# Choice's transpose in a PSUM bank of its own, the first tile's x transposed earlier, and scatters at another place in a pair

## The chip, the cores and the metric

The kernel runs on one core of a Trainium2 chip, as one launch. The metric is the time of that launch on the device, in microseconds; the median of several runs is given.

## What is computed

Three layers follow one another. The first is a retention attention over 8 batches, 8 heads, 576 positions and 64 elements a head. Its result, 4608 rows of 512, goes through a mixture of 8 experts, one for each row, and that result through a soft mixture with 32 slots. Cut to what matters:

```python
Dmat = np.where(rel >= 0, gamma[:, None, None] ** rel, 0.0)
attn = ((scale * q @ k.T) * Dmat) @ v                       # 8 x 8 x 576 x 64
x = attn.transpose(0, 2, 1, 3).reshape(4608, 512)
...
logits = x @ w_gate + modality_bias[modality_id]; e_idx = argmax(logits)
gate_w = softmax(logits)[e_idx]
x = gate_w * (relu(x @ w1[e_idx]) @ w2[e_idx])              # 512 -> 1024 -> 512
...
logits = x @ phi                                            # 4608 x 32
slot_input = softmax(logits, over rows).T @ x               # 32 x 512
slot_out = relu(slot_input @ w1[e]) @ w2[e]                 # 4 slots an expert
out = softmax(logits, over slots) @ slot_out
```

## The kernel before

**Attention.** The 4608 rows are 36 tiles of 128, taken in 18 pairs (a, b). In a pair `emit_v` scales the values (POOL, `vh`, L176), `emit_S`, `emit_cross`, `emit_AV`, `emit_state` and `emit_x` make the rows, `emit_tok` (L226, L227) turns the tile of two pairs ago and writes it to `xd` in DRAM, and `emit_gate` (L222, L223) makes the router's logits. Groups of 4 tiles are then routed by chains of small VectorE instructions that `tick` issues a few at a time: argmax, the rank of a row among the rows of its expert (`rank`, matmuls L253 to L255), the place in the sorted table. `scatter(k)` (POOL, L268, an indirect DMA behind a small memset) writes a tile's row numbers to the table `tb`. There are 36 scatters.

**Slots.** The sorted table is then worked through in slots of 128 rows of one expert; 39 slots are in use. `places` loads a piece of `tb`, `gather` (POOL, L315, L316) fetches the rows into one of three tiles `xg`, `emit_xT` (L464, L466) turns them on TensorE and splits them in a hi part (ScalarE) and a lo part (VectorE), in `xl`. `emit_L1` (L475) is the slot's frame: 24 matmuls of 128x512, with the work of the two slots before hung between them at numbered places (`at(n, ...)`). The places that matter are A = 3 and B = 10. For slot i they issue:

- `emit_hT(i-1)` (L484, L485): turns the hidden layer of the slot before; ScalarE copies one half to hT, VectorE the other.
- `emit_l2(i-1)` (L490): the logits of the soft mixture's choice, `wcur` against hT, into columns 256 to 383 of the PSUM tile `ps_m`, which is one bank.
- `emit_sel(i-2)` (L495) and `emit_zT(i-2)` (L505): choice's maximum and the transpose of z, both into `psz(1)`, columns 384 to 511 of the same `ps_m`.
- `emit_z(i-2)`: `p` (VectorE, L508), `cm` (L509, L510), `cx` (ScalarE's exponential, L511), `cy` (POOL, L514), and the scatter of `cy` to `cs` in DRAM (L515).
- `emit_G(i-2)` (L518): `p` against the hidden layer, into the bank `ps_g`, added up in `Gs` by VectorE (L519).

At place B the order is `emit_l2(i-1)` after `emit_z(i-2)`, then `emit_G(i-2)`. From slot 6 on, a branch (`flush`, L544) in which TensorE, ScalarE and VectorE meet stands between zT and z; it does its work only where the expert changes: `Gs` is turned and multiplied by w2, and `W_mm` (L276) and `W_tr` (L279) make the next `wcur` out of `WT`, 2 MB of w2 from DRAM. Loads of the next expert's weights (`raw`, `wt`, `xw`, `w`) are issued on SP's queue around it, and `cast` and `losplit` (L114, L117) split them into `wh` and `wl`.

**Order of the work.** All of it is written by hand: each engine takes its instructions in the order of the code. The tile framework adds the waits between engines, as it finds them from the tiles that instructions share; the rows of the order below show them in brackets.

**Drain.** After the last slot `drain` finishes the two slots in flight and loads what the soft mixture's second part (`layer1`, `layer2`, `emit_y`) needs that no buffer had room for before; the rest of it was loaded in the slots by `piece`.

Of the kernel before, what the change touches and what calls it, by code (L numbers as in the profile page):

```python
# [17 lines left out]
NPF=6  # L18
# [63 lines left out]
def body(nc,tc,I,O):  # L82
# [8 lines left out]
    with ctx, tc.manual_schedule():  # L91
# [11 lines left out]
        xg2=P0.tile([128,DM],F32,name="xg2"); gT=P0.tile([128,256],F32,name="gT"); SI=P0.tile([128,DM],F32,name="SI")  # L103
        wcur,wnext,wt=(P0.tile([128,256],F32,name=x) for x in ("wcur","wnext","wt"))
# [209 lines left out]
        def gather(i,n=NTOK):  # L314
            g=gi.pop(i); u=uis[i%6]; G_.tensor_copy(out=u,in_=g[:,0:1])  # L315
            G_.indirect_dma_start(out=xg[i%3],out_offset=None,in_=xd[0:n],in_offset=bass.IndirectOffsetOnAxis(ap=u,axis=0),bounds_check=n-1,oob_is_err=False)  # L316
            gi[i]=(g,u)
        def early_places():
            for i in range(NE): places(i,rege(i,TC-1))
        def early_gathers():  # L320
            for i in range(NE): gather(i,6*S)
        emit_v(0); emit_S(0); emit_state(0)
        for P_ in range(NT//2-1):
            a,b=2*P_,2*P_+1; ready=rq and rq[0].__name__=="rank"
            loads(a); loads(b)
# [45 lines left out]
        t8=U(E); ic=U(NSLOT); tg=U(NSLOT); b1=U(NSLOT); n36=wt[0:E,0:36]; r4x=wt[0:E,64:64+4*NSLOT]; r4=r4x.rearrange("p (a b) -> p a b",a=4)  # L371
# [59 lines left out]
        PFt=[[RB if (k,h)==(NPF-1,1) else PF.tile([128,2048],F32,name=f"m{k}_{h}") for h in range(2)] for k in range(NPF)]  # L431
# [30 lines left out]
        def emit_xT(i):  # L462
            ps=ring("ps_xT",0,1,[128,4,128],pl=PX)
            for c in range(4): PE.transpose(out=ps[:,c],in_=xg[i%3][:,c*128:c*128+128],identity=ident)  # L464
            hi=ring("xhi",i,2,[128,4,128],F32R); lo=ring("xlo",i,2,[128,4,128],F32R)
            A.copy(out=hi,in_=ps); V.tensor_tensor(out=lo,in0=ps,in1=hi.bitcast(F32),op=ALU.subtract)  # L466
            xT[i]=(hi,lo)
# [115 lines left out]
        def table(at):  # L583
            at(5,lambda: (mm_r4(),go(c_table)))
            at(14,lambda: [places(j,reg(j,0,[ET.SP],TC-1)) for j in range(NE,6)])
            at(15,lambda: (load_raw(NE),next_WT(NE)))
            at(16,lambda: [gather(j) for j in range(NE,6)])
        def busy(n):
            for _ in range(n): PE.matmul(out=ring("ps_L",0,2,[128,512],pl=PX)[:,0:128],lhsT=sel,rhs=ident,start=True,stop=True)  # L589
        emit_xT(0)  # L590
        for i in range(NSURE):
            slot(i)
            x,h=divmod(i-12,2)
            if 0<=x<NPF: piece(x,[h])
            elif 0<=x-NPF<2 or x==NPF+2 and h==0: SP.dma_start(out=mx[x-NPF][:,2048*h:2048*h+2048],in_=half(MX[x-NPF],h))
        n=nc.values_load(tot[0:1,0:1],engines=[ET.PE,ET.Activation,ET.DVE,ET.Pool,ET.SP],min_val=0,max_val=NSLOT,skip_runtime_bounds_check_because="it is a sum of counts")
        siT=P0.tile([128,4,32],F32,name="siT")
        def drain(i):
# [5 lines left out]
            SP.dma_start(out=XW,in_=half(NPF+3,1))  # L604
# [26 lines left out]
        hT2=[PFt[3][0][:,0:1024].rearrange("p (b f) -> p b f",b=8),WT[1][:,0:1024].rearrange("p (b f) -> p b f",b=8)]  # L631
# [76 lines left out]
```

## Time and profile before

| | |
|---|---|
| median of 3 runs | 699.01 us (697.84 to 699.71) |
| profiled run | 696.97 us, of which the span of the core's work is 695.2 us |
| TensorE busy | 589.1 us, 85% of the span |
| VectorE / POOL / ScalarE busy | 320.2 / 247.0 / 192.7 us |
| granted clock of TensorE, mean | 0.95 |
| attention, slots, drain and second part | to about 184 us, 184 to 601 us, 601 us to the end |

Busy shares are means over stages. What a change in one stage is worth is read from the waits of that stage. All times in the rows further down are counted from the start of the span of the profiled run.

### The profile page before, as it was taken

The page shows a single profiled execution, that of the slowest core. Times are in us where ns is not written, and L with a number is a line of the kernel's source. Part 1 is how long each engine was busy: PE and PEld are TensorE (multiplying, and loading weights), DVE is VectorE, ACT ScalarE, POOL GpSimd, SP SyncE. Part 2 cuts the span into 40 slices and gives each one's busy share as a digit, 9 for nine tenths or more (in the row PEclk, how much of TensorE's full clock was granted, in tenths as well). Part 3 has the DMA queues.
Part 4 walks back from the last instruction along what each step waited for, and adds up shares of the span by engine and source line. Part 5 has one row for each costly group of instructions (what it writes and reads, how often), then busy time and mean ns, then how long its engine had stood idle before and what let it go on. Part 6 is the DMA issues. An engine that isn't in the chain of part 4 may idle for free. (4 is left out here: it accounts for less than half of the span.)

```text
span 695.2 us, 17056 instructions
## 1 busy us (share of the span) xinstructions
PE 589.1 (85%) x5913; PEld 446.0 (64%) x5913; DVE 320.2 (46%) x938; ACT 192.7 (28%) x489; POOL 247.0 (36%) x348
## 2 busy tenths in 40 slices
PE   7889899889798898888988889888779988677984
PEld 5678677777566776666766666566656666453454
DVE  2446445555644444454444563344563444332243
ACT  1132122223412222222222442322442322111333
POOL 3532744444743233333333462243462143110000
PEclk8989999999999999999999989999999999979995
DMA  8999968878316110114333389833475300379978
GB/s 307 402 385 394 362 204 289 293 255 305 113 54 258 32 36 20 35 35 156 135 100 141 135 329 356 347 110 134 138 267 209 140 25 5 135 272 342 390 261 283
DMA packets 45518, 142.33 MB, mean 205 GB/s; under 512 B 11972, under 2 KB 23887, under 8 KB 34128
## 3 DMA queue, kind: packets, MB, share of 16 engines
q1 hardware_dynamic: 39632, 130.44, 51.3%
q0 software_dynamic: 5760, 10.33, 4.7%
q8 instruction: 64, 1.05, 0.6%
q14 instruction: 62, 0.51, 0.2%
HBM read 315.99 MB, written 27.71 MB: 494 GB/s over the span
## 5 line engine op out<-in xcount | busy, mean ns | idle before, releaser
L475 PE MATMUL ps_L<-wh,xl 128*128 128x512 f32 x624 | 214.9, 415 | 2.9 <-DVE xl L466 1.8
L475 PEld LDWEIGHTS ps_L<-wh,xl 128*128 128x128 f32 x624 | 117.2, 193 | 43.9 <-issue 16.8
L475 PE MATMUL ps_L<-wl,xl 128*128 128x512 f32 x312 | 126.0, 404 | 0.0
L514 POOL TENSOR_SCALAR cy<-cx,cm 128x32 f32<-128x32 f32 x39 | 14.5, 371 | 176.8 <-DVE cm L513 171.5
L479 DVE TENSOR_SCALAR hh<-ps_L,gi 128x512 f32<-128x512 f32 x39 | 29.3, 750 | 99.4 <-PE ps_L L475 99.3
L490 PE MATMUL ps_m<-xr__79,wcur 128*32 128x128 f32 x624 | 26.1, 287 | 57.2 <-ACT cx L511 56.2
L475 PEld LDWEIGHTS ps_L<-wl,xl 128*128 128x128 f32 x312 | 60.2, 193 | 13.1 <-issue 0.2
L187 DVE TENSOR_TENSOR st_s<-ps_s,cm 128x512 f32<-128x512 f32 x72 | 46.2, 684 | 37.4 <-PE ps_s L184 25.3
L490 PEld LDWEIGHTS ps_m<-xr__79,wcur 128*32 128x32 f32 x624 | 15.1, 111 | 70.8 <-ACT cx L511 69.3
L499 ACT ACTIVATE z<-ps_m,mt 32x128 f32<-32x128 f32 x39 | 13.9, 358 | 140.9 <-DVE mt L498 133.6
L176 POOL TENSOR_TENSOR vh<-kqv,vtab 128x512 f32<-128x512 f32 x28 | 29.0, 1041 | 59.0 <-PE ps_x L213 42.8
L213 PE MATMUL ps_x<-st_s,vh 128*64 128x128 f32 x576 | 44.1, 283 | 6.8 <-issue 6.5
L515 POOL DMA_INDIRECT cs<-cy,ui x39 | 41.7, 1070 | 15.1 <-POOL cy L514 13.2
L478 ACT ACTIVATE hh<-ps_L,gi 128x512 f32<-128x512 f32 x39 | 26.9, 690 | 72.3 <-PE ps_L L475 68.6
L213 PEld LDWEIGHTS ps_x<-st_s,vh 128*64 128x64 f32 x576 | 33.1, 140 | 19.2 <-issue 18.9
L268 POOL DMA_INDIRECT tb<-m x36 | 35.2, 976 | 26.0 <-DVE m L264 12.8
L484 PE MATMUL ps_h<-cs__113,hh 128*128 128x128 f32 x312 | 40.9, 273 | 1.1 <-DVE hh L479 0.8
L218 DVE TENSOR_TENSOR xT<-ps_x,gt 128x512 f32<-128x512 f32 x36 | 23.2, 686 | 38.2 <-PE ps_x L213 38.0
L316 POOL DMA_INDIRECT xr__79<-xd,ui x28 | 31.0, 1107 | 17.1 <-PE ps_L L475 11.0
L227 ACT COPY xr<-ps_t 128x512 f32<-128x512 f32 x36 | 19.9, 588 | 60.3 <-PE ps_t L226 34.7
L484 PEld LDWEIGHTS ps_h<-cs__113,hh 128*128 128x128 f32 x312 | 35.4, 141 | 1.7 <-DVE hh L479 1.1
L184 PE MATMUL ps_s<-kqv 64*128 64x128 f32 x448 | 34.0, 293 | 0.0
(253 smaller groups left out, 963.5 us busy)
## 6 DMA issues: line engine op xcount, KB each, us to landing
raw<-in_w SPq DMA_DIRECT2D x75, 1024.0 KB
w<-in_w SPq DMA_DIRECT2D x36, 2048.0 KB
xw<-in_w2T SPq DMA_DIRECT2D x36, 1024.0 KB
wt<-in_w2T SPq DMA_DIRECT2D x36, 1024.0 KB
kqv<-in_qkv SPq DMA_DIRECT2D x20, 1024.0 KB
m<-in_m SPq DMA_DIRECT2D x19, 1024.0 KB
w<-in_qkv SPq DMA_DIRECT2D x8, 1024.0 KB
xd<-xr SPq DMA_DIRECT2D x32, 256.0 KB
```

The lines of the kernel that those rows point to most:

```text
L176: G_.tensor_tensor(out=t,in0=kqv[g][:,2].rearrange("p (h d) -> p h d",h=H),in1=bc(vtab[:,pos_(g)],[128,H,D],2),op=ALU.mult)
L184: r=slice(64*h,64*h+64); PE.matmul(out=pss[h][:,p],lhsT=pk(g,0)[r,p],rhs=pk(g,1)[r,p],start=True,stop=True)
L187: V.tensor_tensor(out=st,in0=pss[h],in1=bc(masks[g%NCH],[128,NP,128],1),op=ALU.mult)
L213: PE.matmul(out=xo(g,p,h),lhsT=v[:,2*p+h],rhs=sts[g,h][:,p],start=False,stop=p>1,skip_group_check=True)
L268: nodep(G_.indirect_dma_start(out=tb,out_offset=bass.IndirectOffsetOnAxis(ap=idx[:,k:k+1],axis=0),in_=gk[:,k],in_offset=None),"tb")
L316: G_.indirect_dma_start(out=xg[i%3],out_offset=None,in_=xd[0:n],in_offset=bass.IndirectOffsetOnAxis(ap=u,axis=0),bounds_check=n-1,oob_is_e ...
L475: PE.matmul(out=ps,lhsT=a[:,c],rhs=w[h][:,s],start=n==0,stop=n==11); n+=1; m+=1
L478: if h==0: A.activation(out=d,in_=q,func=AF.Relu,scale=g)
L479: else: V.tensor_scalar(out=d,in0=q,scalar1=0.0,scalar2=g,op0=ALU.max,op1=ALU.mult)
L484: for c in range(4): PE.transpose(out=ps[:,c],in_=hh[i%2][:,2*half+c//2,(c%2)*128:(c%2)*128+128],identity=ident)
L490: PE.matmul(out=ps[32*j:32*j+32],lhsT=w[:,hf*128+32*j:hf*128+32*j+32],rhs=t[:,2*j+hf],start=hf==0,stop=hf==1)
L515: nodep(G_.indirect_dma_start(out=cs,out_offset=bass.IndirectOffsetOnAxis(ap=gi[i][1],axis=0),in_=y,in_offset=None,bounds_check=NTOK-1,oob ...
```

## The change

- `psz(1)` is no longer a part of `ps_m`: it is a PSUM tile `ps_z` of its own, in a bank that was free. `emit_sel` and `emit_zT` write there and `emit_z` reads there.
- The kernel no longer sets the size of the scratch for the descriptors of indirect DMAs (8192), but takes the default.
- `scatter`: 3 of a pair (4 once) are issued right behind the pair's two `emit_v`, where 4 stood at the pair's end. The 12 of the last three groups come one after the other: 8 just ahead of the slots, 4 in the first slot, with nothing of POOL's between.
- The first tile's `emit_xT(0)` stands in the last pair, behind `W_mm`; `cast(1)` a pair earlier; `losplit(1)` wholly on POOL, behind the first gathers; the rank of the last group but one behind the gate; `mm_r4` and `c_table` at place 4 of the second slot, not 5.
- Tiles are packed to make room: `xg2`, `gT`, `wcur`, `wnext` and `wt` in one tile (`m6`, seen as `m_81` below), `xr` in a part of `xr_`. The piece `m3_1` (1 MB) has no buffer of its own any more: it takes `WT[1]` and is loaded in the drain, ahead of `XW`, not in the slots.

```diff
-        xg2=P0.tile([128,DM],F32,name="xg2"); gT=P0.tile([128,256],F32,name="gT"); SI=P0.tile([128,DM],F32,name="SI")
-        wcur,wnext,wt=(P0.tile([128,256],F32,name=x) for x in ("wcur","wnext","wt"))
+        M6=P0.tile([128,1536],F32,name="m6"); xg2=M6[:,0:DM]; gT,wcur,wnext,wt=(M6[:,DM+256*j:DM+256*j+256] for j in range(4)); SI=P0.tile([128,DM],F32,name="SI")
...
-            xr=A1.tile([128,DM],F32,name="xr",bufs=2); A.copy(out=xr,in_=xp)
+            xr=XR[:,1024+DM*(g%2):1024+DM*(g%2)+DM]; A.copy(out=xr,in_=xp)
...
             emit_v(b); emit_v(a+2)
+            if a>13:
+                for _ in range(4 if a==30 else 3):
+                    if scat: scatter(scat.pop(0))
...
             tick(14)
-            if a>13:
-                for _ in range(4):
-                    if scat: scatter(scat.pop(0))
...
-                cast(0); losplit(0,[0,1],V); losplit(0,[2,3],G_)
+                cast(0); losplit(0,[0,1],V); losplit(0,[2,3],G_); cast(1)
...
-        emit_v(b); early_gathers(); emit_S(a); emit_cross(a); emit_cross(b)
+        emit_v(b); early_gathers(); losplit(1,range(4),G_); emit_S(a); emit_cross(a); emit_cross(b)
...
-        emit_tok(a-2); emit_tok(b-2); tick(6); emit_S(b); emit_gate(a//2-1); cast(1); losplit(1,[0],V); losplit(1,[1,2,3],G_)
-        emit_AV(a); emit_AV(b); emit_x(a); emit_x(b)
-        tick(20); logit(a-2); logit(b-2); tick(1,False)
-        W_mm(PS1.tile([128,256],F32,name="ps_w",tag="ps_s0")); emit_tok(a); emit_tok(b); emit_gate(a//2,True)
-        W_tr(PS1.tile([128,256],F32,name="ps_wt",tag="ps_s1"),[wcur])
-        tick(20)
-        while scat: scatter(scat.pop(0))
+        emit_tok(a-2); emit_tok(b-2); tick(7); emit_S(b); emit_gate(a//2-1)
+        emit_AV(a); emit_AV(b); emit_x(a); emit_x(b); tick(20)
+        W_mm(PS1.tile([128,256],F32,name="ps_w",tag="ps_s0")); emit_xT(0,PS1.tile([128,4,128],F32,name="ps_xT0",tag="ps_s1"))
+        logit(a-2); logit(b-2); emit_tok(a); emit_tok(b); emit_gate(a//2,True); tick(1,False)
+        W_tr(PS1.tile([128,256],F32,name="ps_wt",tag="ps_s0"),[wcur])
...
-        def psz(j,w=128): return psm[:,256+128*j:256+128*j+w]
+        def psz(j,w=128): return (ring("ps_z",0,1,Z,pl=PX) if j else psm[:,256:384])[:,:w]
...
-            at(5,lambda: (mm_r4(),go(c_table)))
+            at(4,lambda: (mm_r4(),go(c_table)))
...
-        emit_xT(0)
+        tick(20)
+        while scat: scatter(scat.pop(0))
...
-            if 0<=x<NPF: piece(x,[h])
+            if 0<=x<NPF: (x,h)==(3,1) or piece(x,[h])
...
-            SP.dma_start(out=XW,in_=half(NPF+3,1))
+            piece(3,[1]); SP.dma_start(out=XW,in_=half(NPF+3,1))
...
-    nc=bacc.Bacc("TRN2",target_bir_lowering=False,num_devices=1,dynamic_dma_scratch_size=8192)
+    nc=bacc.Bacc("TRN2",target_bir_lowering=False,num_devices=1)
```

In the order of the changed kernel, lines have moved: L505 is L502 there, L490 is L487, L518 is L515, L475 is L472, L464 is L320, L544 is L541, and L253, L276, L279 and L222 are one less. The rows name the line, the matmul's output and inputs, its shape, and in brackets the engines whose semaphores it waits for (Activation is ScalarE, Pool is POOL).

TensorE at place B of an ordinary slot with the branch, before: the last L1 matmul ahead of it, zT, `l2`, `G`, and L1 again.

```order
L475 MATMUL ps_L_2497<-wh_69,xl 128x512
L505 MATMUL ps_m<-cs__113,z_2505 128x128 [waits DVE_49]
L490 MATMUL ps_m<-xr__79,wcur 32x128 [waits Activation_49]
L490 MATMUL ps_m<-xr__79,wcur 32x128 x7
L518 MATMUL ps_g_2508<-hh_2486,p_2493 32x257
L544 UNCONDITIONAL_BRANCH
L518 MATMUL ps_g_2508<-hh_2486,p_2493 32x257 x3
L475 MATMUL ps_L_2497<-wh_69,xl 128x512
```

The same place in the changed kernel (`m_81` is `wcur` in the packed tile).

```order
L472 MATMUL ps_L_2442<-wh_69,xl 128x512
L502 MATMUL ps_z_2447<-cs__109,z_2451 128x128 [waits DVE_49]
L487 MATMUL ps_m<-xr__79,m_81 32x128 [waits Activation_49]
L487 MATMUL ps_m<-xr__79,m_81 32x128
L487 MATMUL ps_m<-xr__79,m_81 32x128 [waits DVE_49]
L487 MATMUL ps_m<-xr__79,m_81 32x128 x5
L515 MATMUL ps_g_2454<-hh_2431,p_2438 32x257 [waits DVE_49]
L541 UNCONDITIONAL_BRANCH
L515 MATMUL ps_g_2454<-hh_2431,p_2438 32x257 x3
L472 MATMUL ps_L_2442<-wh_69,xl 128x512
```

zT now writes `ps_z`, and `l2`'s waits are spread over two of its matmuls. `G` waits for VectorE by itself.

TensorE between attention and slots, before: the last tiles are turned, gated, `W_tr` is made, and the first tile's x is turned and meets L1.

```order
L226 MATMUL ps_t<-cs__113,xT 128x128 x8
L222 MATMUL ps_m<-xT,wg 32x256 x4
L279 MATMUL ps_wt<-cs__113,wt 128x128 [waits Activation_49]
L279 MATMUL ps_wt<-cs__113,wt 128x128
L464 MATMUL ps_xT_2509<-cs__113,xr__79 128x128 [waits DMASW4_49,PE_49]
L464 MATMUL ps_xT_2509<-cs__113,xr__79 128x128 x3
L475 MATMUL ps_L_2497<-wh_69,xl 128x512 [waits Activation_49]
L475 MATMUL ps_L_2497<-wh_69,xl 128x512 [waits DVE_49]
```

In the changed kernel the first tile's x is turned behind `W_mm`.

```order
L275 MATMUL ps_w<-wt_77,phi 32x256 x7
L320 MATMUL ps_xT_2360<-cs__109,xr__79 128x128 [waits DMASW0_49,PE_49]
L320 MATMUL ps_xT_2360<-cs__109,xr__79 128x128 x3
L232 MATMUL ps_m<-cs__109,ls 128x8 [waits Activation_49]
L232 MATMUL ps_m<-cs__109,ls 128x8
L225 MATMUL ps_t<-cs__109,xT 128x128 [waits DVE_49]
L225 MATMUL ps_t<-cs__109,xT 128x128 x3
L225 MATMUL ps_t<-cs__109,xT 128x128 [waits DVE_49]
L225 MATMUL ps_t<-cs__109,xT 128x128 x3
L221 MATMUL ps_m<-xT,wg 32x256 x4
```

The end of the same stretch in the changed kernel, from `W_tr` (its input is `wt` in the packed tile) to the first L1 matmuls.

```order
L278 MATMUL ps_wt<-cs__109,m_81 128x128 [waits PE_49]
L278 MATMUL ps_wt<-cs__109,m_81 128x128
L472 MATMUL ps_L_2442<-wh_69,xl 128x512 [waits PE_49]
L472 MATMUL ps_L_2442<-wh_69,xl 128x512 [waits DVE_49]
L232 MATMUL ps_m<-cs__109,m_81 128x8 [waits DVE_49]
L232 MATMUL ps_m<-cs__109,m_81 128x8
```

Four transposes (L464, now L320) have moved from between `W_tr` and L1 to behind `W_mm`, ahead of the last tiles; the rank's matmuls, which stood ahead of `W_mm`, now stand between the gate (L221) and `W_tr`.

## Rows read from the trace of the kernel before

**Rows 1.** the page's head, and TensorE's busy time (share) and instructions.

```profile
span 695.2 us, 17056 instructions
...
PE 589.1 (85%) x5913; PEld 446.0 (64%) x5913; DVE 320.2 (46%) x938; ACT 192.7 (28%) x489; POOL 247.0 (36%) x348
```

**Rows 2.** waits, 203 to 600 us: engine, line, releaser: us in total, times, longest.

```profile
PE ps_m L490 <- ACT cx L511: 52.1, 37, 3.0
...
DVE p L508 <- PEq L544: 8.2, 25, 0.3
```

**Rows 3.** timeline of TensorE, one slot: start, length (us), [idle before, releaser].

```profile
280.35 0.27 PE L505 MATMUL ps_m<-cs__113,z 128*128 128x128 f32 x1
281.85 0.65 PE L490 MATMUL ps_m<-xr__79,wcur 128*32 128x128 f32 x16 [1.23 <-ACT cx L511]
282.31 0.62 PE L518 MATMUL ps_g<-hh,p 128*32 128x257 f32 x8
```

**Rows 4.** timeline of VectorE, ScalarE and POOL in the same slot.

```profile
279.21 0.69 DVE L485 COPY xr__79<-ps_h 128x512 f32<-128x512 f32 x1
...
280.82 0.19 DVE L508 COPY p<-ps_m 128x32 f32<-128x32 f32 x1 [0.32 <-PEq L544]
...
281.61 0.19 ACT L511 ACTIVATION_READ_ACCUMULATOR cx<-ps_m,cm 128x1 f32 x1
...
282.37 0.37 POOL L514 TENSOR_SCALAR cy<-cx,cm 128x32 f32<-128x32 f32 x1 [4.83 <-DVE cm L513]
```

**Rows 5.** timeline of VectorE and TensorE in the last slot.

```profile
618.86 0.19 DVE L508 COPY p<-ps_m 128x32 f32<-128x32 f32 x1 [0.76 <-PE ps_m L505]
...
619.11 0.64 PE L518 MATMUL ps_g<-hh,p 128*32 128x257 f32 x8 [0.28 <-DVE p L508]
```

**Rows 6.** timeline of TensorE, a slot without the branch.

```profile
221.42 0.64 PE L490 MATMUL ps_m<-xr__79,wcur 128*32 128x128 f32 x16 [1.06 <-ACT cx L511]
```

**Rows 7.** timeline of TensorE, an expert change and the drain.

```profile
413.02 0.64 PE L490 MATMUL ps_m<-xr__79,wcur 128*32 128x128 f32 x16 [3.05 <-ACT cx L511]
...
612.74 1.08 PE L490 MATMUL ps_m<-xr__79,wcur 128*32 128x128 f32 x16 [4.12 <-ACT cx L511]
```

**Rows 8.** timeline of TensorE and VectorE, from attention to the slots.

```profile
179.89 0.18 PE L253 MATMUL ps_m<-m 128*128 128x32 bf16 x1 [0.95 <-DVE m L247]
...
185.46 0.50 PE L475 MATMUL ps_L<-wh,xl 128*128 128x512 f32 x1 [1.04 <-ACT xl L466]
187.79 0.49 PE L475 MATMUL ps_L<-wh,xl 128*128 128x512 f32 x1 [1.83 <-DVE xl L466]
...
187.11 0.63 DVE L466 TENSOR_TENSOR xl<-ps_xT,xl 128x512 fp32r<-128x512 f32 x1
```

**Rows 9.** windows: busy us of each engine, granted clock, DMA share, GB/s.

```profile
400.00:405.00 5.00, 5.00 (x35) 3.53 (x36) 3.83 (x9) 2.64 (x6) 3.12 (x3) 0.66 0.65 264
...
410.00:415.00 5.00, 1.98 (x26) 1.39 (x27) 1.59 (x8) 2.70 (x7) 2.39 (x3) 0.89 1.00 413
415.00:420.00 5.00, 5.00 (x20) 3.96 (x20) 2.41 (x4) 0.69 (x1) 2.09 (x2) 0.77 1.03 414
515.00:520.00 5.00, 3.84 (x29) 2.67 (x30) 2.94 (x10) 1.53 (x5) 2.70 (x3) 0.66 0.94 349
620.00:625.00 5.00, 4.96 (x43) 3.21 (x42) 1.75 (x8) 0.57 (x2) 1.38 (x2) 1.00 0.10 37
```

**Rows 10.** timeline of TensorE at the second expert change.

```profile
439.55 1.07 PE L276 MATMUL ps_m<-wt,phi 128*32 128x256 f32 x16 [0.94 <-DMA wt<-in_w2T]
```

**Rows 11.** waits, whole span.

```profile
POOL vh L176 <- PE ps_x L213: 48.6, 11, 8.1
```

**Rows 12.** line L268: nanoseconds least, median, most; first and last start.

```profile
L268 POOL DMA_INDIRECT tb<-m x36: 954/960/1169, 75.0 to 199.8; - x36
```

**Rows 13.** timeline of POOL, the last four scatters.

```profile
196.01 0.97 POOL L268 DMA_INDIRECT tb<-m  x1 [4.25 <-DVE SI L385]
...
199.84 0.97 POOL L268 DMA_INDIRECT tb<-m  x1 [0.22 <-issue]
```

More of the change, by code (lines that the diff above doesn't have):

```diff
@@ L317, in gather, with emit_xT @@
             gi[i]=(g,u)
+        xT={}
+        def emit_xT(i,ps=None):
+            ps=ring("ps_xT",0,1,[128,4,128],pl=PX) if ps is None else ps; o=1024*(i%2)
+            for c in range(4): PE.transpose(out=ps[:,c],in_=xg[i%3][:,c*128:c*128+128],identity=ident)
+            hi,lo=(XL.bitcast(F32R)[:,o+512*k:o+512*k+512].rearrange("p (c t) -> p c t",c=4) for k in range(2))
+            A.copy(out=hi,in_=ps); V.tensor_tensor(out=lo,in0=ps,in1=hi.bitcast(F32),op=ALU.subtract)
+            xT[i]=(hi,lo)
         def early_places():
@@ L370, in body @@
         cnt,nf,beg,np_,nn=(U(1) for _ in range(5)); nb=U(E); ee=U(E+2); end=ee[:,0:1]; total=ee[:,E+1:]; tot=T("tot",[1,1],I32)
-        t8=U(E); ic=U(NSLOT); tg=U(NSLOT); b1=U(NSLOT); n36=wt[0:E,0:36]; r4x=wt[0:E,64:64+4*NSLOT]; r4=r4x.rearrange("p (a b) -> p a b",a=4)
+        t8=U(E); ic=U(NSLOT); tg=U(NSLOT); b1=U(NSLOT); n36=wnext[0:E,0:36]; r4x=wnext[0:E,64:64+4*NSLOT]; r4=r4x.rearrange("p (a b) -> p a b",a=4)
         ef=U(NSLOT+1,False); sb=U(NSLOT,False); rem=T("rem",[128,NSLOT]); ec=U(NSLOT)[0:1]; ns=U(NSLOT)[0:1]
@@ L430, in body @@
         w2p=[w2[:,4*h:4*h+4].rearrange("p c d -> p (c d)") for h in range(2)]
-        PFt=[[RB if (k,h)==(NPF-1,1) else PF.tile([128,2048],F32,name=f"m{k}_{h}") for h in range(2)] for k in range(NPF)]
+        PFt=[[{(NPF-1,1):RB,(3,1):WT[1]}.get((k,h)) or PF.tile([128,2048],F32,name=f"m{k}_{h}") for h in range(2)] for k in range(NPF)]
         mt[NPF]=raw
@@ L450, in body @@
         Z=[128,128]
-        def psz(j,w=128): return psm[:,256+128*j:256+128*j+w]
+        def psz(j,w=128): return (ring("ps_z",0,1,Z,pl=PX) if j else psm[:,256:384])[:,:w]
         def psg(w): return ring("ps_g",0,1,[128,512],pl=PX)[:,:w]
-        xT={}; hT={}; l2={}; zz={}; pp={}
+        hT={}; l2={}; zz={}; pp={}
         for j in range(2):
             ring("pad",0,1,Z)
-            for k,x in enumerate(("xhi","xlo")): rings[x,j]=XL.bitcast(F32R)[:,1024*j+512*k:1024*j+512*k+512].rearrange("p (c t) -> p c t",c=4)
             ring("mt",j,2,[128,4]);
@@ L461, in emit_pad @@
             G_.tensor_scalar(out=ring("pad",0,1,Z),in0=iota,scalar1=rem[:,i:i+1],scalar2=-1e30,op0=ALU.is_ge,op1=ALU.mult)
[L462 to L467, printed above, removed]
         def emit_L1(i,hooks):
@@ L630, in body, with h2 @@
         ph={}
-        hT2=[PFt[3][0][:,0:1024].rearrange("p (b f) -> p b f",b=8),WT[1][:,0:1024].rearrange("p (b f) -> p b f",b=8)]
+        hT2=[PFt[3][0][:,0:1024].rearrange("p (b f) -> p b f",b=8),None]
+        def h2(r,x): return hT2[0][:,4*x:4*x+4] if r==0 else (M6[:,1024:1536],SI)[x].rearrange("p (b f) -> p b f",b=4)
         def layer1(r,c,first,last):
@@ L637, in relu @@
         def relu(r):
-            hm=WT[1][:,1024:2048]
+            hm=M6[:,0:1024]
             for x in range(2): V.tensor_scalar(out=hm[:,x*512:x*512+512],in0=ph[r,x],scalar1=0.0,scalar2=rows4[:,r:r+1],op0=ALU.max,op1=ALU.mult)
@@ L644, in turn @@
                 for c in range(4): PE.transpose(out=ps[:,c],in_=hm[:,x*512+c*128:x*512+c*128+128],identity=ident)
-                A.copy(out=hT2[r][:,4*x:4*x+4],in_=ps)
+                A.copy(out=h2(r,x),in_=ps)
         identr=T1.tile([128,128],F32R,name="identr"); A.copy(out=identr,in_=ident)
@@ L668, in layer2 @@
             for j in range(4):
-                PE.matmul(out=pos[dh][32*j:32*j+32],lhsT=hT2[r][:,fc,32*j:32*j+32],rhs=w[:,j*256:j*256+256],start=k==0,stop=k==15)
+                PE.matmul(out=pos[dh][32*j:32*j+32],lhsT=h2(r,fc//4)[:,fc%4,32*j:32*j+32],rhs=w[:,j*256:j*256+256],start=k==0,stop=k==15)
         shls={}
```

## The prediction

> **What bounds the kernel now.** I read the page's totals first. TensorE is busy 589.1 us of a 695.2 us span [rows 1], so about 106 us are its idle time, and only what shortens that idle time can shorten the kernel. The table of waits over the slots (203 to 600 us) then says what ends it: 37 times, 52.1 us in all, the first matmul of the choice logits `emit_l2` (L490) waits for ScalarE's exponential `cx` (L511) [rows 2]. No other wait of TensorE there comes near this. So half of the idle time is one wait, met once in every slot.
>
> One slot shows how it is built [rows 3, 4]. TensorE ends the transpose of z (L505) at 280.35+0.27 = 280.62 and then stands for 1.23 us. VectorE takes `p` out of it (280.82 to 281.01) and ScalarE `cx`, whose last part ends at 281.80; `l2` starts at 281.85 and `G` (L518) at 282.31. `l2` reads nothing of `cx`: it multiplies hT by wcur, and the later copy of hT ended at 279.21+0.69 = 279.90, before z's transpose began. It writes columns 256 to 383 of `ps_m`, and `cx` reads columns 384 to 511, which lie in the same bank. The wait is thus one of place, if the change's first part is understood rightly.
>
> The Trainium skill bears on this reading: its page "PSUM — Partial Sum Buffer", section "PSUM bank collisions raise a hardware error", says that two engines must be kept apart on a bank and 32-partition quadrant whichever columns each touches. The trace agrees that the wait is there with disjoint columns (1.23 us in rows 3). By the page a bank of its own frees `l2` and the sum below stands; were only addresses kept apart, the wait would have another cause and the slots' term would be 0.
>
> **The change, part by part.** The sum is made against the profiled run, 696.97 us (span 695.2); the median of the runs shown, 699.01, is 2.0 above it, and I add that at the end.
>
> *1. Bank of its own for psz(1).* In the new order `l2` waits only for the two copies of hT, and `G` gets a wait of its own for VectorE, that is for `p`. In the slot shown `l2` can start at about 280.66. `G` then needs `l2` to be through (0.46 from its start, 281.85 to 282.31 in rows 3) and `p` to be done (281.01). The last slot, which has no `l2` between, shows the price of the second: `p` ends at 618.86+0.19 = 619.05 and `G` starts at 619.11, 0.06 later [rows 5]. So `G` starts at about the later of 281.12 and 281.07, against 282.31: 1.19 us. I take 1.10, since `p` starts after a branch that TensorE and VectorE meet in (VectorE waits 0.3 us for TensorE's queue at most, 25 times [rows 2]) and I cannot see whether TensorE's own side of it holds `l2`. If it does, `l2` goes after `p` and about half, 0.6, is won. Slots without that branch wait 1.06 [rows 6]: 1.0 each, four of them. Slots at an expert change have the same 1.30 between `p`'s end and `G` (281.01 to 282.31 here). 33 × 1.10 + 4 × 1.0 = 40.3. In the drain `l2` waits 4.12 us for `cx` [rows 7], most of it for work ahead of `p`; there the clock is low, so I put the 1.19 a little higher, at 1.4. Together −41.7, with bounds of −23 (0.6 a slot) and −46 (1.24 a slot).
>
> What is late next? POOL. Its chain in a slot (cy, scatter of cs, its landing, ui, gather) leaves it idle 4.83 us before `cy` [rows 4]; a slot 1.1 us shorter still leaves 3.7. Nothing follows from that.
>
> *2. First tile's transposes in the last pair.* TensorE stands 1.04 us and 1.83 us for the hi and lo halves of the first tile's x, and 0.95 us for the rank's input [rows 8]. The first two go: the transposes and both copies are done while the gate's work runs. The lo half, at 187.11, sat on VectorE behind the routing and the memsets [rows 8]. The rank moves behind the gate, but its matmul now waits for ScalarE's copy of the last gate logits, so part of the 0.95 comes back: 0.5 to 1.0. Net −2.8; bounds 0 (all of it returns as a wait of the rank and of W_tr behind it) and −4.8 (all three go, and the rest of 1.0 us elsewhere in the routing's chain).
>
> *3. Clock.* The granted clock is lower at the expert changes: 0.66 in 400 to 405 and in 515 to 520, 0.89 and 0.77 in 410 to 420 [rows 9]. A clock of 0.66 over 5 us means that 3.4 us of it ran at the lower level (1.2 GHz, full is 2.4), and at half speed 5 × 0.34 = 1.7 us are lost. TensorE had stood before: the one at 413.02 ends a pause of 3.05 us [rows 7], from which part 1 takes 1.1. I count two stretches avoided, −3.4, as an estimate from the two rows of 0.66; bounds 0 and all four windows, 5 × (0.34+0.34+0.11+0.23) = −5.1.
>
> *4. What eats gains.* At expert changes the DMA engines are the limit: share 1.00 in 410 to 415 [rows 9], and at 439.55 TensorE waits 0.94 us for `wt` from DRAM [rows 10]. Slots that come earlier wait longer there: +1.1 at one change; bounds 0 and +4.4 (two slots' gain at each of two changes). In the drain 1 MB more is to be loaded. At the 413 GB/s of a window with share 1.00 that is 1.05 MB / 413 = 2.5 us, and in 620 to 625, before the tail begins, the share is only 0.10 [rows 9]; the tail uses the piece after others. +0.5, bounds 0 and +2.5.
>
> *5. At nothing.* Scatters behind the scaled values: POOL waits 48.6 us for TensorE in that stage before `vh` [rows 11], so three scatters of 0.96 us [rows 12] fit. Were that cover gone, TensorE would wait 3 × 1.3 = 4 us a pair. Twelve scatters now stand in one burst ahead of the fourth tile's gather. Before, the last four waited 4.25 us for VectorE and ended at 199.84+0.97 = 200.81 [rows 13]; twelve at (199.84−196.01)/3 = 1.28 from about 187 (the routing ahead of them is through before the lo half at 187.11) end at 202 to 203. The gather behind them moves by some 2 us, and its tile is wanted a slot later; 0, bound +2. The losplit's fourth piece on POOL goes to a queue that then waits for VectorE anyway. Packing of tiles, the size of the descriptor scratch (scatters keep an even pace, no row shows a wait for room) and the hook at 4 change no wait that a row shows: 0.
>
> Sum: −41.7 −2.8 −3.4 +1.1 +0.5 = −46.3, so the profiled run is about 651, and the median 699.0 − 46.3 = 652.7.
>
> **Rivals.**
> *A, half the gain.* The branch, or `p`, takes the place of `cx`: 0.6 a slot, 22 us, and no clock won; with part 2 about 675. For it: VectorE waits for TensorE's queue at the branch. Against it: 0.06 us after `p` in the last slot. Chance 0.10.
> *B, the wait is not of place.* `l2` still waits for something late (wcur in the packed tile, or VectorE's reading of the logits). Then only part 2 counts, 696 to 699. Against it: TensorE's order names only hT's copies, which were done at 279.90. 0.03.
> *C, slower: POOL becomes the pace.* Its chain per slot has 4.83 us of room now [rows 4]. Were its scatter and gather stretched by more than 4.83 us together, POOL would set a slot longer than now and the kernel would be slower from there on: at 5.0 us more, 37 × 0.17 = 6 us, 705; at 6.0 us, 742. For it: VectorE's l and Gs move to where POOL issues. Against it: 36 scatters lie between 954 and 1169 ns, many beside VectorE's work [rows 12]. 0.02. The Trainium skill has such a mechanism (page "SBUF — State Buffer", section "SBUF: two separate sides"): POOL cannot write descriptors while VectorE holds the shared port; it gives about 620 ns growing to 3100, so two issues a slot would grow by 5.0 us, an estimate from that page, and rival C's 705 would come true. The trace does not agree so far, since no scatter of these 36 takes more than 1.17 us.
> *D, more of it eaten at the expert changes and in the drain.* Part 1 at 1.0 a slot (−38), part 2 at −1, no clock won, part 4 at its bounds (+7): −32, about 667. 0.10.
> My forecast: 0.75.
>
> **How the numbers follow.** About 0.3% (2 us) is what a measurement of this kernel can tell from no change. Forecast, A and D all lie far below the time before, B on its edge: faster 0.95, same 0.03, slower 0.02. Range: the forecast's bounds taken together, not all at once, reach from 643 (−46, −4.8, −5.1) to 660; with D it goes to 667. I give 644 to 668, which leaves out most of A, and B and C.
>
> **What would show it.** Right: the wait of `l2` for `cx` gone from the table; `G` 0.1 us after `p`; ordinary slots of 8.65 us instead of 9.75; `cy` preceded by some 3.7 us of idle POOL; no wait for xl before the first L475; granted clock higher in the slices of the expert changes; TensorE's busy time nearly the same. Wrong: slots above 9.2 (A); the wait of `l2` under another name (B); `cy`, ui or the gather with no idle time before it and scatters above 3 us (C); waits for raw, wt or the drain's pieces that grow by more than 4 us (D).

## The result, and the profile after

The changed kernel takes 655.47 us (median of 4 runs, 654.73 to 656.91). Beside it the kernel before took 699.36 us (4 runs, 697.84 to 700.17). The ratio is 0.9377, interval 0.9353 to 0.9402: 43.9 us faster. 652.7 was predicted, with a range of 644 to 668.

The profiled execution took 656.91 us, 1.4 above its median; that of before lies 2.4 below its own. So the two traces differ by only 695.2 − 655.1 = 40.1 us, and the accounts below explain these 40.1. First the page's head and TensorE's row, which answer to [rows 1]: TensorE is busy 2.9 us less, its idle time falls from 106 to 69 us.

```profile
span 655.1 us, 17029 instructions
...
PE 586.2 (89%) x5913; PEld 446.0 (68%) x5913; DVE 314.9 (48%) x937; ACT 192.7 (29%) x489; POOL 248.2 (38%) x349
```

The table of waits from 200 to 560 us, after, in the order of [rows 2] (engine, line, releaser: us in total, times, longest). `l2` is now L487 and `cx` L508. No row names `l2` waiting for `cx`; the 52.1 us are gone. What `l2` still waits for is ScalarE: its queue (ACTq) at the branch, at expert changes, and twice its copy there (2.0 us in all); and once the routing (`rem`).

```profile
POOL cy L511 <- DVE cm L510: 118.3, 33, 7.7
...
POOL ui L314 <- DMA cs<-cy,ui: 32.5, 31, 3.7
...
PE ps_m L487 <- ACTq L541: 10.7, 6, 4.0
...
PE ps_m L487 <- DVE rem L412: 6.3, 1, 6.3
```

One ordinary slot of the changed kernel in the timeline, which answers to [rows 3, 4].

```profile
272.08 0.27 PE L502 MATMUL ps_z<-cs__109,z 128*128 128x128 f32 x1
272.50 0.64 PE L487 MATMUL ps_m<-xr__79,m 128*32 128x128 f32 x16
272.94 0.64 PE L515 MATMUL ps_g<-hh,p 128*32 128x257 f32 x8
...
272.39 0.19 DVE L505 COPY p<-ps_z 128x32 f32<-128x32 f32 x1 [0.17 <-PE ps_z L502]
...
273.93 0.37 POOL L511 TENSOR_SCALAR cy<-cx,cm 128x32 f32<-128x32 f32 x1 [3.74 <-DVE cm L510]
274.66 1.07 POOL L512 DMA_INDIRECT cs<-cy,ui  x1 [0.36 <-POOL cy L511]
```

zT ends at 272.08+0.27 = 272.35 and `l2` starts 0.15 later, where 1.23 us stood. `G` follows 0.44 behind `l2`, and 0.36 behind the end of `p` (272.58): `l2` sets it, not `p`. POOL is idle 3.74 us before `cy`; 3.7 was predicted.

Stage by stage, by TensorE's instructions in the two traces, in us. px are the matmuls of `emit_x` (L213, now L212), and the last px are those of the last tile; zT 0, zT 1 and so on are the transposes of z, one for each slot. Stretches run from start to start, those that begin or end with a zT from its end. The term of −2.8 of step 2 stands in two rows, since one of its two waits for `xl`, 1.83 us [rows 8], lay behind the first L1.

| stretch | before | after | difference | predicted |
|---|---|---|---|---|
| attention, to the last px | 177.24 | 169.51 | −7.7 | 0 |
| last px to the first L1 | 8.22 | 7.81 | −0.4 | −1.0 |
| first L1 to the end of the first zT | 24.87 | 32.49 | +7.6 | −1.8 −1.1 |
| 28 slots without an expert change | 275.0 | 244.8 | −30.2 | −30.4 |
| 8 slots at the two expert changes | 110.1 | 103.4 | −6.7 | −8.8 −3.4 +1.1 |
| drain, zT 36 to zT 38 | 23.36 | 17.02 | −6.3 | −1.4 |
| tail | 76.4 | 80.0 | +3.6 | +0.5 |
| sum | | | −40.1 | −46.3 |

The plain slots came as predicted. Attention gained 7.7 us that nobody had foreseen, and the first stretch of the slots lost as much; these two cancel. In all, the traces gained 6.2 us less than predicted. The experiments take this apart.

### The profile page after: what moved, and what is told of

It reads as the page before. It is cut to its first block, busy times and chain, and to the rows that moved or that the text cites. A ratio compares the mean times of both kernels' runs of the same rounds, so it can differ in the third digit from the quotient of the medians.

```text
span 655.1 us, 17029 instructions
## 1 busy us (share of the span) xinstructions
PE 586.2 (89%) x5913; PEld 446.0 (68%) x5913; DVE 314.9 (48%) x937; ACT 192.7 (29%) x489; POOL 248.2 (38%) x349
## 5 line engine op out<-in xcount | busy, mean ns | idle before, releaser
L472 PE MATMUL ps_L<-wh,xl 128*128 128x512 f32 x624 | 215.0, 415 | 0.0
L472 PEld LDWEIGHTS ps_L<-wh,xl 128*128 128x128 f32 x624 | 116.9, 193 | 40.2 <-issue 16.8
L472 PE MATMUL ps_L<-wl,xl 128*128 128x512 f32 x312 | 125.7, 403 | 0.0
L472 PEld LDWEIGHTS ps_L<-wl,xl 128*128 128x128 f32 x312 | 60.2, 193 | 13.2
L496 ACT ACTIVATE z<-ps_z,mt 32x128 f32<-32x128 f32 x39 | 14.0, 358 | 136.6 <-DVE mt L495 118.3
L487 PE MATMUL ps_m<-xr__79,m 128*32 128x128 f32 x624 | 27.0, 288 | 24.0 <-ACTq L541 10.7
L212 PE MATMUL ps_x<-st_s,vh 128*64 128x128 f32 x576 | 41.8, 285 | 1.9 <-issue 1.2
L481 PE MATMUL ps_h<-cs__109,hh 128*128 128x128 f32 x312 | 40.8, 273 | 2.9 <-DVE hh L476 2.9
L487 PEld LDWEIGHTS ps_m<-xr__79,m 128*32 128x32 f32 x624 | 16.4, 112 | 37.2 <-issue 20.7
L226 ACT COPY xr__79<-ps_t 128x512 f32<-128x512 f32 x36 | 20.2, 587 | 70.7 <-DMA xd<-xr__79 25.1
L212 PEld LDWEIGHTS ps_x<-st_s,vh 128*64 128x64 f32 x576 | 33.0, 142 | 10.9 <-issue 10.5
L475 ACT ACTIVATE hh<-ps_L,gi 128x512 f32<-128x512 f32 x39 | 27.0, 691 | 39.0 <-PE ps_L L472 37.3
L481 PEld LDWEIGHTS ps_h<-cs__109,hh 128*128 128x128 f32 x312 | 35.3, 141 | 3.5 <-DVE hh L476 3.3
L183 PE MATMUL ps_s<-kqv 64*128 64x128 f32 x448 | 36.2, 303 | 0.3 <-issue 0.3
```

Of the source, the lines that this page charges most:

```text
L183: r=slice(64*h,64*h+64); PE.matmul(out=pss[h][:,p],lhsT=pk(g,0)[r,p],rhs=pk(g,1)[r,p],start=True,stop=True)
L212: PE.matmul(out=xo(g,p,h),lhsT=v[:,2*p+h],rhs=sts[g,h][:,p],start=False,stop=p>1,skip_group_check=True)
L472: PE.matmul(out=ps,lhsT=a[:,c],rhs=w[h][:,s],start=n==0,stop=n==11); n+=1; m+=1
L475: if h==0: A.activation(out=d,in_=q,func=AF.Relu,scale=g)
L481: for c in range(4): PE.transpose(out=ps[:,c],in_=hh[i%2][:,2*half+c//2,(c%2)*128:(c%2)*128+128],identity=ident)
L487: PE.matmul(out=ps[32*j:32*j+32],lhsT=w[:,hf*128+32*j:hf*128+32*j+32],rhs=t[:,2*j+hf],start=hf==0,stop=hf==1)
```

## Experiments

**Chips.** e1 to e4 ran on one chip, where the kernel before took 698.39 us (19 runs, 691.51 to 702.74); e5 to e8 on a chip with the same number, before 697.36. e10 and e11 ran on a second (before 683.73), e12 and e13 on a third (before 680.26). Each ratio is taken on its own chip. The chip of the result above is not on record; by its 699.36 us before it is counted here with the first.

**e1: the bank alone, in the kernel before.**

```diff
-        def psz(j,w=128): return psm[:,256+128*j:256+128*j+w]
+        def psz(j,w=128): return (ring("ps_z",0,1,Z,pl=PX) if j else psm[:,256:384])[:,:w]
```

> Theory (the bank carries most of the gain): ordinary slots go from 9.75 to 8.67 us, so 28 of them give 30, the slots at the two expert changes give some 5 more, the drain about 1: 661 to 664 us; attention and the first L1 (185.5 us) stay where they were. Rival (the bank gives the slots' 30 only, and what else was won at the expert changes and in the drain comes from the piece that is no longer loaded there): 667 to 669 us.

Measured: 655.71 us, ratio 0.9408 (0.9367 to 0.9449), that is −42.7 us, at least 5 more than was expected. The 28 plain slots lose 30.1 us, the drain 6.3, as in the changed kernel, where 1 was expected of the drain; the slots at the expert changes lose 8.9.

**e3: everything but the bank** (the changed kernel with the line of e1 put back).

```diff
-        def psz(j,w=128): return (ring("ps_z",0,1,Z,pl=PX) if j else psm[:,256:384])[:,:w]
+        def psz(j,w=128): return psm[:,256+128*j:256+128*j+w]
```

> The changed kernel with choice's transpose back in the bank of the logits. Theory (bank 36 us, all the rest together 6 to 8 us): 690 to 693 us, the wait of l2 for cx back at 1.2 us a slot. Rival (the rest is worth nothing by itself): 697 to 700 us.

Measured: 694.38 us, ratio 0.9962 (0.9921 to 1.0002). That lies between the theory and the rival: the rest brings some 4 us, not clear of nothing. In its table of waits (205 to 600 us) the old wait is back whole:

```profile
PE ps_m L487 <- ACT cx L508: 51.9, 37, 2.9
```

e1 and e3 together show that the one line carries the gain: with it alone the time is that of the whole change, without it nearly that of before. The line gives `psz(1)` a tile and a bank of its own at once, so the two runs don't tell which of the two the wait followed.

**e2: the scatters' place alone, in the kernel before.**

```diff
             emit_v(b); emit_v(a+2)
+            if a>13:
+                for _ in range(4 if a==30 else 3):
+                    if scat: scatter(scat.pop(0))
...
             tick(14)
-            if a>13:
-                for _ in range(4):
-                    if scat: scatter(scat.pop(0))
```

> Theory (the scatters' place in the pair is what made attention shorter): TensorE reaches the last pair 7 to 8 us earlier, as in the changed kernel, but eight scatters instead of four now stand between attention and the slots, so part of it is given back there: 692 to 697 us. Rival (attention is shorter for another reason, the size of the scratch or the new order of the last pairs): the pairs' times equal those of the kernel before to within 1 us, and the whole stays at 699.

Measured: 694.44 us, ratio 0.9947 (0.991 to 0.9984). By its trace (the fastest of its ten runs, 688.07 us) the last px comes 8.9 us sooner (7.9 of it from pair 7 on: pair 7 to 16 in 83.19 us for 88.05, and 9.55 for 12.54 behind it), and half of that is lost in the first slot (first L1 to first `l2` 21.43 for 17.23). This is what the theory expected. The prediction had put the place at nothing; it is worth some 4 us.

**e4: the size of the descriptor scratch** (the changed kernel with `dynamic_dma_scratch_size=8192` again).

> The changed kernel with the scratch for descriptors at 8192 as before. Theory (the size does nothing): 655 us within 1.5, attention's end unchanged. Rival (the default size is what shortened attention): TensorE reaches the last pair 7 to 8 us later and the whole takes 660 to 663 us.

Measured: 654.65 us, ratio 0.9395 (0.9345 to 0.9444). The size does nothing, as predicted. So e4 also serves as a second trace of the changed kernel.

**e5 and e8: without scatters, and without the last twelve** (in the changed kernel). This is e5; e8 puts `if k<24:` ahead of the line instead, and both fill `cs` by two transfers at tile 20.

```diff
-            nodep(G_.indirect_dma_start(out=tb,out_offset=bass.IndirectOffsetOnAxis(ap=idx[:,k:k+1],axis=0),in_=gk[:,k],in_offset=None),"tb")
+            pass
```

> The changed kernel without any of its 36 scatters to the table (so the slots work on padding rows and the output is not the reference's); the rows of cs are filled with zeros instead, 0.6 MB in attention. Theory (a scatter on POOL holds TensorE up, in attention and again at the start of the slots): the last pair begins 5 us or more before the changed kernel's 169.5, and the first matmul of the choice logits comes 16 to 17 us after the first L1 matmul instead of 23. Rival (the pause in the first slot is the copy of hT, which now shares its place with rows on their way to DRAM): the 23 us stay, though nothing is scattered.

> The changed kernel with the 24 scatters in the pairs, but without the 12 in a row around the start of the slots (the rows of 12 tiles are missing from the table, so the output is not the reference's); cs filled with zeros as above. Theory: attention as in the changed kernel (169.5 us), and 16 to 17 us from the first L1 matmul to the first choice logits. Rival (hT's place): 23 us.

Measured, one run each: 634.64 and 645.95 us, against 654.65 for e4 on this chip. Without any scatter the pairs 7 to 16 take 72.06 us instead of the 83.44 after; without the last twelve they take 80.79. (e6 and e7, run beside them with all scatters, take 81.05 and 81.91.) From the first L1 to the first `l2`: 14.40 and 13.53, against 22.99. So both lengths belong to the scatters, and the second to the twelve that stand in one burst. Both are shorter than the 16 to 17 us that were expected.

**e6: `xr` in tiles of its own again** (e4 with this).

```diff
-            xr=XR[:,1024+DM*(g%2):1024+DM*(g%2)+DM]; A.copy(out=xr,in_=xp)
+            xr=A1.tile([128,DM],F32,name="xr",bufs=2); A.copy(out=xr,in_=xp)
```

> The changed kernel with the rows on their way to DRAM in tiles of their own again, apart from hT (and the scratch for descriptors at 8192, which makes the room). Theory (the scatters hold TensorE up): no change against the same kernel with the shared place, 653 to 656 us, and still 22 to 23 us from the first L1 matmul to the first choice logits. Rival (hT's place): 646 to 649 us, and 16 to 17 us between these two.

Measured: 653.0 us, ratio 0.9356 (0.9284 to 0.9428). To the first `l2` it takes 21.75 us, near the theory's 22 to 23 and far from the rival's 16 to 17. From the first L1 to the end of the first zT it takes 29.4 us, e4 32.9: the shared place of `xr` and `hT` (both in columns 1024 to 2047 of `xr_`) may be some 3.5 of the 7.6 us lost there, by one trace of each. In the total it is inside the intervals.

**e7: bank and scatters' place in the kernel before** (the edits of e1 and e2).

> The kernel before with the bank and the scatters' new place in the pair, and nothing else. Theory (terms add: the bank's 42.7 and the scatter's 4): 650 to 653 us, with attention as short as in the changed kernel. Rival (what the scatters give in attention they take back in the first slots, so that only the bank counts): 655 to 657 us.

Measured: 649.64 us (649.12 to 650.27), ratio 0.9318 (0.925 to 0.9386), at the theory's lower end: the lowest time on this chip of a kernel that leaves nothing out. The intervals of e7, e6, e4 and the change overlap, so that it beats the change is likely there and not shown.

**e10: the scatters one by one** (e7, with one scatter ahead of, between and behind the two `emit_v`).

```diff
-            emit_v(b); emit_v(a+2)
+            sc(1); emit_v(b); sc(1); emit_v(a+2); sc(2 if a==30 else 1)
```

> The kernel before with the bank, and the scatters of a pair put one by one around its two scaled values instead of three in a row behind them. Theory (several scatters in a row hold TensorE up, a single one between other work does not): attention from its pair 7 to its pair 16 goes from 82 us towards the 72 us that it takes without scatters, 75 to 78; the whole 643 to 647 us. Rival (each scatter costs TensorE the same wherever it stands, or POOL's scaled values become late): 82 to 84 us there, and 649 to 652 in all.

Measured: 639.49 us, ratio 0.9372 (0.9334 to 0.9409). Pairs 7 to 16 take 73.95 us. That is below the 75 to 78 expected, but e11, on the same chip with three scatters in a row, takes 73.37 there. So the run can't tell the theories apart.

**e11: without the load moved into the drain** (1 MB left out).

```diff
-            piece(3,[1]); SP.dma_start(out=XW,in_=half(NPF+3,1))
+            mt.setdefault(3,{})[1]=WT[1]; SP.dma_start(out=XW,in_=half(NPF+3,1))
```

> The changed kernel without the 1 MB load that it moved into the drain (that part of the second layer's weights is then wrong, and with it the output). Theory (the load lies ahead of what the tail waits for): from the last z to the first matmul of the tail 10 to 11 us instead of 12.5, the whole 653 to 654 us. Rival (it is hidden, the tail's longer start comes from the shorter drain alone): 12.5 us and 655 to 656 us.

Measured: 639.82 us, ratio 0.9375 (0.9328 to 0.9422). The 653 to 656 us expected were meant for the first chip. From zT 38 to the tail's first matmul it takes 11.24 us, between the theory and the rival, against 12.52 after, but e4 and e12, which make the load, take 11.22 and 11.97. Over all traces with the bank, the kernels with this load in the drain take 11.2 to 12.5 us there, those without it 9.7 to 11.2. So the load may cost about 1 us; it is not settled.

**e12 and e13: the changed kernel again, beside e10 again**, on one chip.

> The changed kernel once more, beside the next one on the same chip, since the last two ran on a chip that showed no hold of TensorE by scatters. Theory (the hold belongs to the chip): the time from pair 7 to pair 16 of attention and the one from the first L1 matmul to the first choice logits go together, 83 and 22 to 23 us where the kernel before takes some 697, or 73 and 14 to 16 us where it takes some 684; the ratio to the kernel before is 0.935 to 0.942 on either. Rival (the changed kernel's first slot is held up on every chip): 22 to 23 us even where attention is short.

> The bank with the scatters one by one, beside the changed kernel on the same chip. Theory (the rest of the change costs more than it brings): 2 to 6 us less than the changed kernel, from the end of the slots to the tail and, where scatters hold TensorE, in attention too. Should the chip hold TensorE: if only scatters in a row do so, 75 to 78 us from pair 7 to pair 16; if each does, 82 to 84. Rival: the two kernels agree within 1.5 us.

Measured: 639.88 us (6 runs, 638.75 to 646.75), ratio 0.9419 (0.937 to 0.9468), and 639.06 us (636.23 to 640.3), ratio 0.9391 (0.9352 to 0.943). The first theory holds: on this chip, before 680.26 us, the changed kernel's pairs 7 to 16 take 72.06 us with all scatters in place, and 13.83 pass from the first L1 to the first `l2`. Between the two kernels the rival holds: they take the same time within 1 us. e13 takes 5.1 us longer to its first `l2` than e12 and gets 5.0 back by the fifth zT (36.53 us from the first for 41.50). So there e7 with its scatters spread does as well as the whole change; whether spreading helps where scatters hold TensorE, no run shows.

## Why the prediction was right, step by step

**Step 1, the slots: right in mechanism and size.** Plain slots went from 9.75 to 8.67 us (8.65 predicted), 28 of them −30.2 against −30.4. `l2` had read and written nothing of `cx`; a tile in another bank freed it. `G` starts 0.36 us behind `p`, not 0.1 as the signs had it, since `l2` now sets it. The Trainium skill's page "PSUM — Partial Sum Buffer", section "PSUM bank collisions raise a hardware error", keeps two engines apart on a bank and 32-partition quadrant whatever columns they touch; the kernels e1 and e3 agree, 1.1 us a slot.

**Steps 1, 3 and 4, the expert changes: −6.7 instead of −11.1.** One such slot in the trace after: TensorE, then ScalarE.

```profile
385.98 0.27 PE L502 MATMUL ps_z<-cs__109,z 128*128 128x128 f32 x1
390.30 1.08 PE L487 MATMUL ps_m<-xr__79,m 128*32 128x128 f32 x16 [4.05 <-ACTq L541]
...
388.02 2.18 ACT L113 CAST wh<-raw 128x512 fp32r<-128x512 f32 x4 [2.66 <-DMA raw<-in_w]
```

And the like slot before, that of [rows 7] whose `l2` starts at 413.02.

```profile
409.74 2.18 ACT L114 CAST wh<-raw 128x512 fp32r<-128x512 f32 x4 [0.65 <-DMA raw<-in_w]
```

Before, the cast ended at 411.92 and `l2` came 1.10 us behind it, with `p` and `cx` between; after, it ends at 390.20 and `l2` comes 0.10 behind it. So the bank gave its 1.0 us here too. But the cast stands ahead of `l2` either way, and it waits for `raw` 2.0 us longer than before. That is the DMA term of step 4, as expected of slots that come earlier: it was sized at 1.1. Most is missing at the first change (−1.6 for its four slots; the second gave −5.0; the bank alone was counted at −4.4 for each). But the size differs from trace to trace. e4, the same kernel but for the scratch, shows at the same cast:

```profile
387.02 2.18 ACT L113 CAST wh<-raw 128x512 fp32r<-128x512 f32 x4 [1.35 <-DMA raw<-in_w]
```

Its eight slots give −9.0. With the bank this wait is 1.27 to 3.23 us in all traces, without it 0.31 to 0.65; on the first chip the eight slots take 101.1 to 103.4 us with the bank and 106.7 to 110.1 without. So it is shown that the wait grows, and the −6.7 is partly the luck of two traces. The clock term did not come. The windows after, in the columns of [rows 9] (granted clock, DMA share and GB/s stand last):

```profile
385.00:390.00 5.00, 1.25 (x6) 0.70 (x5) 1.87 (x7) 2.34 (x5) 2.62 (x4) 0.88 1.01 377
390.00:395.00 5.00, 4.70 (x31) 3.24 (x32) 3.08 (x7) 1.68 (x5) 2.77 (x3) 0.50 1.02 419
...
485.00:490.00 5.00, 3.68 (x31) 2.74 (x32) 2.90 (x7) 2.70 (x7) 3.13 (x4) 0.78 1.03 410
490.00:495.00 5.00, 5.00 (x28) 4.25 (x28) 1.80 (x7) 1.00 (x4) 1.06 (x3) 0.88 0.99 396
```

Behind the pause of 4.05 us the clock is 0.50 for five us, the lower level (1.2 GHz) throughout, where [rows 9] had 0.66. At the second change it fell less, 0.78 and 0.88. The estimate of −3.4 took the pauses as shorter, and one of them became longer. It did not come in e4 either, where the pause is 2.75 us: 0.70 in 390 to 395 and 0.66 in 485 to 490.

**Step 2, first tile's transposes: the two waits of [rows 8] for `xl` are gone, but ahead of the first L1 TensorE found others.** Timeline of TensorE, after:

```profile
174.07 0.63 PE L320 MATMUL ps_xT<-cs__109,xr__79 128*128 128x128 f32 x4 [1.53 <-DMA xr__79<-xd,ui]
...
177.03 0.18 PE L252 MATMUL ps_m<-m 128*128 128x32 bf16 x1 [0.49 <-ACT m L222]
...
177.33 0.71 PE L472 MATMUL ps_L<-wh,xl 128*128 128x512 f32 x2
```

The moved transpose waits 1.53 us for its own gather, and the rank 0.49 for the gate logits (0.5 to 1.0 foreseen). The step counted no wait for the gather, which was the missing item: these two make 2.02 us, as much as the 0.95 and 1.04 before, and the first L1 comes 0.4 us nearer to the last px where 1.0 was counted. The wait of 1.83 us, behind the first L1, is won; the burst of step 5 covers that gain.

**Step 5, "at nothing": wrong in both its places.** It priced a scatter at POOL's time for it, 0.96 us, and looked for cover on POOL. That stayed true (least, median, most of the 36 after: 955, 970 and 1170 ns). The price fell on TensorE, which the step had put at nothing. The windows of pairs 7 to 16 (from left: length, TensorE's busy us and matmuls, ..., clock, DMA share, GB/s) of before, of after, of e5 without scatters, and of e12, the changed kernel on the third chip:

```profile
76.65:164.70 88.05, 78.11 (x1298) 64.22 (x1294) 46.71 (x130) 19.58 (x47) 43.40 (x66) 0.98 0.78 272
```

```profile
76.27:159.71 83.44, 77.35 (x1299) 65.27 (x1295) 46.53 (x130) 20.21 (x50) 43.48 (x65) 0.96 0.82 295
```

```profile
77.65:149.71 72.06, 71.18 (x1298) 61.56 (x1294) 46.26 (x130) 19.53 (x48) 20.08 (x39) 1.00 0.94 341
```

```profile
78.44:150.50 72.06, 71.18 (x1299) 61.61 (x1295) 46.23 (x130) 19.50 (x47) 41.68 (x63) 1.00 0.92 329
```

The same matmuls keep TensorE busy 6 to 7 us longer, and it stands idle 5 to 9 us more, where scatters run on the first chip; on the third the scatters cost nothing that shows here. The clock is part of it, 0.98 and 0.96, but not all: in e6 and e8, at 1.00, TensorE is busy 74.90 and 75.12 us. 23 scatters start in this stretch before as after; in threes behind the `emit_v` they cost 4.6 us less than in fours at a pair's end. (e1, with the attention of before, takes 91.90 us; all kernels with threes on this chip take 80.8 to 84.4.) Behind pair 16, where three stood before and none now, 2.7 us more are won: that is the −7.7, but for the 0.4 by which pair 7 starts sooner. The loss of 7.6 behind it is the burst of twelve: without these, e8 takes 21.18 us in that stretch (though 10.47 in the one ahead of it), where before took 24.87 (and 8.22) and the prediction had 2.9 less. Timelines of ScalarE, VectorE and TensorE in the first slot, after ("remote": the profile finds no releaser nearer):

```profile
194.18 0.59 ACT L482 COPY xr__79<-ps_h 128x512 f32<-128x512 f32 x1 [11.96 <-remote]
...
188.43 0.75 DVE L476 TENSOR_SCALAR hh<-ps_L,gi 128x512 f32<-128x512 f32 x1 [1.77 <-remote]
196.97 0.69 DVE L482 COPY xr__79<-ps_h 128x512 f32<-128x512 f32 x1 [7.80 <-remote]
...
200.00 0.18 DVE L412 SCALAR_TENSOR_TENSOR rem<-SI,ps_m 128x43 f32<-128x43 f32 x1
...
189.23 0.66 PE L481 MATMUL ps_h<-cs__109,hh 128*128 128x128 f32 x4 [2.90 <-DVE hh L476]
...
200.32 1.08 PE L487 MATMUL ps_m<-xr__79,m 128*32 128x128 f32 x16 [6.31 <-DVE rem L412]
```

Both copies of hT start 7 to 8 us behind the matmuls that they read (L481, through at 186.33 and 189.89), the routing's last values stand behind VectorE's copy, and `l2` behind them. The burst ran from 179.81 to 194.87. Behind the pause of 6.31 us the granted clock is 0.55 in 200 to 205. On the third chip the same burst leaves the copies where they belong, and what remains is the wait for the fourth tile's gather, for which the step had a bound of +2; ScalarE, then TensorE in e12:

```profile
178.15 0.59 ACT L482 COPY xr__79<-ps_h 128x512 f32<-128x512 f32 x1 [4.18 <-PE ps_h L481]
...
182.91 0.64 PE L487 MATMUL ps_m<-xr__79,m 128*32 128x128 f32 x16 [1.08 <-DVE rem L412]
...
196.84 0.66 PE L320 MATMUL ps_xT<-cs__109,xr__79 128*128 128x128 f32 x4 [3.21 <-DMA xr__79<-xd,ui]
```

The copy starts 0.1 us behind its matmuls (through at 178.07). The gather's wait is 3.21 us, and the stretch from the first zT to the fifth is 5.0 us longer than after, so the bound was too small.

Why the first chip holds TensorE so and the others don't is open. That the scatters are the cause there is shown by e5 and e8; the way from a scatter to a matmul is not. The Trainium skill's page "SBUF — State Buffer", section "SBUF: two separate sides", has POOL's descriptors late while VectorE holds the shared port; these traces don't show it, since the scatters keep 955 to 1170 ns on POOL.

**The drain: −6.3 for −1.4.** The wait of 4.12 us before `l2` [rows 7] became one of 1.32. VectorE in the drain, before:

```profile
606.75 0.29 DVE L497 TENSOR_REDUCE mt<-ps_m 128x1 f32<-128x128 f32 x1 [4.61 <-issue]
...
611.71 0.19 DVE L508 COPY p<-ps_m 128x32 f32<-128x32 f32 x1 [2.65 <-issue]
```

After, the same two instructions, and TensorE's `l2`:

```profile
566.61 0.29 DVE L494 TENSOR_REDUCE mt<-ps_z 128x1 f32<-128x128 f32 x1 [2.79 <-PE ps_h L481]
...
569.07 0.19 DVE L505 COPY p<-ps_z 128x32 f32<-128x32 f32 x1
...
569.80 1.08 PE L487 MATMUL ps_m<-xr__79,m 128*32 128x128 f32 x16 [1.32 <-PEq L541]
```

VectorE had stood 4.61 and 2.65 us for nothing that the profile shows ("issue"), and waits 2.79 and 0 now. The kernels with the bank take 16.7 to 18.1 us here, those without 23.0 to 23.6, so it comes with the bank. Why VectorE stands less, no run tested. Of the 6.3 us, 2.9 are given back at the tail's first matmul, which waits for the last loads (before, 9.58 us lay between zT 38 and it; after, 12.52):

```profile
587.64 1.07 PE L635 MATMUL q_h<-wh,siT 128*32 128x512 f32 x2 [5.60 <-DMA xw<-in_m]
```

**The rivals.** A (half the gain): no, `G` starts 0.6 us behind zT's end; by A 1.1 of the 1.7 would have stayed. B: no, e3. C: no, POOL keeps 3.74 us of room in the slot shown and its scatter of cs takes 1.07. D: partly, at the first expert change and the tail; its 667 asked for 1.0 a slot and 7 us eaten, where the slots kept 1.08 and the drain gave 4.9 us that no case had counted.

So the sum was near for two reasons. The one term that carried 30 us was exact. The others missed by −7.7 (attention), +10.5 (first slot), −4.9 (drain), +4.4 (expert changes), +3.1 (tail) and +0.6 us (last px to first L1), minus where the kernel was faster than predicted, which leaves +6 in the traces. That these cancel so far is luck: the scatters that brought both the −7.7 and the loss in the first slot stood in the sum at nothing. The medians lie 3.8 us further apart than the traces, hence 655.5 for 652.7.

## What to carry to other kernels

If an instruction waits on one that shares no data with it, look at whose bank both touch: a spare bank was worth 1.08 us in each of 28 plain slots, and one line did it. Where a wait is removed, look for what stands just ahead of it on the other engine (here the cast behind `raw`), since that sets the new end. An edit that costs nothing on its own engine can still have its price on another; run it alone, as e2, and on more than one chip.

## What was not expected of the hardware

- The same kernel takes 698 us on one chip and 680 to 684 on two others; the traces of the changed kernel on the first and the third (spans of 655.1 and 639.8 us) part in the stretches with scatters (pairs 7 to 16: 83.44 and 72.06; first L1 to the end of the first zT: 32.49 and 21.49), of which the third gives back 5.0 by its late gather (first zT to the fifth: 36.53 and 41.50).
- On the first chip the same 1298 matmuls keep TensorE busy 75 to 80 us beside scatters, over all its traces, and 71.18 us without, while the scatters on POOL take 955 to 1170 ns, as they did before.
- At the entry to the drain VectorE stood 4.61 and 2.65 us for nothing that the profile shows, and in every kernel with the bank less (2.4 to 3.2 us, then 0.1).
